# SwiGLU feed-forward: the first loads reordered, and half of the first rows projected before the other half is transposed

## The chip, the cores and the metric

The kernel runs on one core of one Trainium2 chip. The metric is the device time of one execution in microseconds (us), the median over several runs. Beside the times there is one profiled execution of the kernel, whose trace gives the start and the length of every instruction and transfer.

## What is computed

A SwiGLU feed-forward layer in bf16, with x of 2048 rows by 640, w_gate and w_up of 640 by 1536 and w_down of 1536 by 640:

```python
def reference(x, w_gate, w_up, w_down):
    g = silu(x @ w_gate)
    u = x @ w_up
    return (g * u) @ w_down
```

## The kernel before

**Tiles.** The 2048 rows are worked through in four blocks (`sb`) of 512 rows. F = 1536 is cut into 12 slices (`fc`) of 128, and D = 640 into 5 slices (`kd`) of 128. For each block and each `fc`, TensorE projects the transposed block `xT` with the gate slice into a PSUM tile `pg` and with the up slice into `pu`, five matmuls each, one per `kd`, with the weights stationary and 512 columns (rows of x) moving. ScalarE takes SiLU of `pg` into `sg`, VectorE multiplies by `pu` into `aT`. When the 12 slices are done, the block is projected with w_down: `po_t` holds the last 128 output columns transposed, `po_a` the first 512 output columns for each 128 rows. The last block makes the last 128 rows of those columns in `po_b`.

**The start.** For the first block, x comes in four chunks of 128 rows (`x_sb`, chunks 0 to 3) and TensorE transposes it: `transpose_chunk` makes five 128x128 transposes into a PSUM tile `pt`, and a copy brings `pt` to `xT`. Ahead of that TensorE multiplies a tile of ones by itself 20 times (`warm`, tile `pw`); these matmuls, called fillers here, produce nothing that is used. For the other three blocks `xT` is written by transposing transfers.

**Order of the first loads.** Two queues issue transfers, that of SyncE (SP) and that of ScalarE (ACT). Before the change each takes: x chunk (0 on SP, 2 on ACT), x chunk (1 on SP, 3 on ACT), its part of the first gate slice `wg_sb` (kd 0 to 2 on SP, kd 3 and 4 on ACT), its part of the first up slice `wu_sb` in the same way. All further weights go on SP alone: gate and up in chunks of 2, 3, 3 and 3 slices (`W_CHUNKS`), then w_down, then the transposing transfers. Eight semaphores are shared out to the transfers in turn, so the ninth transfer in program order waits at its queue until the first has landed, the tenth for the second, and so on. ScalarE, after its last start transfer, loads its function table (L89) and makes one small SiLU.

**Order on TensorE at the start.** It is written out by hand and held by `keep_order`: 20 fillers; transposes of chunks 0, 2, 1 and 3; two fillers; `pg` for rows 0 to 383; `pg` for rows 384 to 511; `pu` for all 512 rows; then the slices 1 to 11 in the regular form. Three of the chunks are copied to `xT` whole by VectorE, chunk 3 by VectorE (2 of 5 kd) and ScalarE (3 of 5). PSUM has four buffers under the tag `gu` (`pw`, `pg`, `pu`) and two each under `po_a` and `po_b`, which the `pt` tiles of the start borrow.

Of the kernel before, what the change touches and what calls it, by code (L numbers as in the profile page):

```python
# [10 lines left out]
def _body(  # L11
# [8 lines left out]
    nc = tc.nc  # L20
    P = nc.NUM_PARTITIONS
# [5 lines left out]
    B, S0, D = x.shape  # L27
    F = w_gate.shape[1]
    S = B * S0
# [3 lines left out]
    KD = D // P  # L33
    KF = F // P
    S_BLK = 512
    NSB = S // S_BLK
    SUB = S_BLK // P
    DA = 512
    Q = 32
    N_WARM = 20  # L40
    W_CHUNKS = [(0, 1), (1, 3), (3, 6), (6, 9), (9, 12)]
    assert D % P == 0 and F % P == 0 and S % S_BLK == 0 and D > DA and SUB >= 2

    consts = ctx.enter_context(tc.tile_pool(name="consts", bufs=1))
    work = ctx.enter_context(tc.tile_pool(name="work", bufs=3))
# [8 lines left out]
    wg_sb = consts.tile([P, KD, F], bf16)  # L54
    wu_sb = consts.tile([P, KD, F], bf16)
# [7 lines left out]
    wg_v = w_gate.rearrange("(kd p) f -> p kd f", p=P)  # L63
    wu_v = w_up.rearrange("(kd p) f -> p kd f", p=P)
    wd_v = w_down.rearrange("(kf p) d -> p kf d", p=P)

    def wslice(a, b):
        return slice(a * P, b * P)

    def load_w(eng, dst, src, a, b):  # L70
        eng.dma_start(out=dst[:, :, wslice(a, b)], in_=src[:, :, wslice(a, b)])

    def load_x(eng, c0, c1):
        eng.dma_start(out=x_sb[:, c0:c1, :], in_=x_v[:, c0:c1, :])
# [4 lines left out]

    queues = (nc.sync, nc.scalar)  # L80
    halves = ((0, KD // 2 + 1), (KD // 2 + 1, KD))
    for c in (0, 1):
        for i, eng in enumerate(queues):
            load_x(eng, c + 2 * i, c + 2 * i + 1)
    for dst, src in ((wg_sb, wg_v), (wu_sb, wu_v)):
        for eng, (k0, k1) in zip(queues, halves):
            eng.dma_start(out=dst[:, k0:k1, wslice(0, 1)], in_=src[:, k0:k1, wslice(0, 1)])
    load_w(nc.sync, wg_sb, wg_v, *W_CHUNKS[1])
    nc.scalar.activation(silu_first[:], ones[:, 0:1], ACT.Silu)  # L89
    load_w(nc.sync, wu_sb, wu_v, *W_CHUNKS[1])  # L90
    for a, b in W_CHUNKS[2:]:
# [9 lines left out]
    def warm(n):  # L101
        for _ in range(n):
            nc.tensor.matmul(  # L103
                pw[:, 0:P], lhsT=ones[:], rhs=ones[:], start=True, stop=True
            )

    def keep_order(engine):

        traced = [i for i in nc.cur_bb.bb.instructions if i.engine == engine]
        for a, b in zip(traced, traced[1:]):  # L110
            tc.add_manual_dep(
                b,
                a.name,
                mybir.DependencyInfo(
                    mybir.DependencyClass.NoSync, mybir.DependencyReason.DATA
                ),
                reason="keep_order",
            )

    def transpose_chunk(c, parts):  # L120
        c_sl = slice(c * P, (c + 1) * P)
        for copy, tag, k0, k1 in parts:
            pt = psum.tile([P, k1 - k0, P], bf16, tag=tag, name="pt")
            for kd in range(k0, k1):
                nc.tensor.transpose(  # L125
                    out=pt[:, kd - k0, :],
                    in_=x_sb[:, c, kd * P : (kd + 1) * P],
                    identity=ident[:],
                )
            copy(out=xT[:, k0:k1, c_sl], in_=pt[:])  # L130

    def proj(ps, w_sb, fc, sb, c0, c1):
        for kd in range(KD):
            nc.tensor.matmul(  # L134
                ps[:, c0:c1],
                lhsT=w_sb[:, kd, fc * P : (fc + 1) * P],
                rhs=xT[:, kd, sb * S_BLK + c0 : sb * S_BLK + c1],
                start=(kd == 0),
                stop=(kd == KD - 1),
            )  # L140

    for sb in range(NSB):
        s_sl = slice(sb * S_BLK, (sb + 1) * S_BLK)
        for fc in range(KF):
            pg = psum.tile([P, S_BLK], f32, tag="gu", name="pg", bufs=4)
            pu = psum.tile([P, S_BLK], f32, tag="gu", name="pu", bufs=4)
            if sb == 0 and fc == 0:
                h = (SUB - 1) * P
                warm(N_WARM)
                for n, c in enumerate((0, 2, 1)):  # L150
                    transpose_chunk(
                        c, [(nc.vector.tensor_copy, ("po_a", "po_b")[n % 2], 0, KD)]
                    )
                transpose_chunk(
                    SUB - 1,
                    [
                        (nc.vector.tensor_copy, "po_b", 0, 2),
                        (nc.scalar.copy, "po_a", 2, KD),
                    ],
                )  # L160
                warm(2)
                proj(pg, wg_sb, fc, sb, 0, h)
                proj(pg, wg_sb, fc, sb, h, S_BLK)
                proj(pu, wu_sb, fc, sb, 0, S_BLK)
                keep_order(mybir.EngineType.PE)
                keep_order(mybir.EngineType.Activation)
            else:
                proj(pg, wg_sb, fc, sb, 0, S_BLK)
                proj(pu, wu_sb, fc, sb, 0, S_BLK)
            sg = work.tile([P, S_BLK], f32)  # L170
            nc.scalar.activation(sg[:], pg[:], ACT.Silu)  # L171
            nc.vector.tensor_tensor(  # L172
                out=aT[:, fc, s_sl], in0=sg[:], in1=pu[:], op=ALU.mult
            )


        n_t = (SUB if sb < NSB - 1 else SUB - 1) * P
        po_t = psum.tile([P, n_t], f32, tag="po_b", name="po_t")
        for kf in range(KF):
            nc.tensor.matmul(  # L180
                po_t[:],
                lhsT=wd_sb[:, kf, DA:D],
                rhs=aT[:, kf, sb * S_BLK : sb * S_BLK + n_t],
                start=(kf == 0),
                stop=(kf == KF - 1),
            )
        ot_t = outp.tile([P, n_t], bf16, name="ot_t")
        ot_q = outp.tile([P, n_t], bf16, name="ot_q")
        nc.scalar.copy(ot_t[:], po_t[:])  # L189
        nc.vector.transpose(out=ot_q[:], in_=ot_t[:])  # L190
        for q in range(P // Q):
            nc.scalar.dma_start(
                out=out2[
                    sb * S_BLK : sb * S_BLK + n_t, DA + q * Q : DA + (q + 1) * Q
                ].rearrange("(i r) c -> r i c", r=Q),
                in_=ot_q[q * Q : (q + 1) * Q, :].rearrange("r (i c) -> r i c", c=Q),
            )

        for j in range(SUB):
            s0 = sb * S_BLK + j * P  # L200
            last = sb == NSB - 1 and j == SUB - 1
            po_a = psum.tile([P, DA], f32, tag="po_a", name="po_a")
            for kf in range(KF):
                nc.tensor.matmul(  # L204
                    po_a[:],
                    lhsT=aT[:, kf, s0 : s0 + P],
                    rhs=wd_sb[:, kf, 0:DA],
                    start=(kf == 0),
                    stop=(kf == KF - 1),
                )  # L210
            ot = outp.tile([P, DA], bf16, name="ot")
            nc.scalar.copy(ot[:], po_a[:])  # L212
            nc.sync.dma_start(out=out2[s0 : s0 + P, 0:DA], in_=ot[:])
            if last:
                po_b = psum.tile([P, D - DA], f32, tag="po_b", name="po_b")
                for kf in range(KF):
                    nc.tensor.matmul(  # L217
                        po_b[:],
                        lhsT=aT[:, kf, s0 : s0 + P],
                        rhs=wd_sb[:, kf, DA:D],  # L220
                        start=(kf == 0),
                        stop=(kf == KF - 1),
                    )
                ot_b = outp.tile([P, D - DA], bf16, name="ot_b")
                nc.vector.tensor_copy(out=ot_b[:], in_=po_b[:])  # L225
                nc.scalar.dma_start(out=out2[s0 : s0 + P, DA:D], in_=ot_b[:])
# [76 lines left out]
def kernel(tc, *args):  # L303
    _body(tc, *args)
    tc.close()
    tc.compile()
    _trim(tc.nc)
# [30 lines left out]
```

## Time and profile before

| | us |
|---|---|
| median of 8 runs | 164.35 |
| lowest and highest of them | 163.86, 165.48 |
| the profiled execution, its own time | 163.86 |
| its span, first to last instruction | 162.5 |
| TensorE busy | 159.2 (98% of the span) |
| ScalarE busy | 42.2 |
| VectorE busy | 37.9 |

How to read a profile: PE is a matmul on TensorE, PEld a weight load on TensorE, DVE is VectorE, ACT ScalarE, POOL GpSimd, SP SyncE; SPq and ACTq are the issuing of transfers on their queues. In the timeline a line gives start and length of a merged run of equal instructions, then the engine, the line of code, the operation, the tiles out<-in, the shape and the count (x20). Matmuls are pipelined, so the length of one (219 ns for 128 columns, 379 ns for 512) is longer than the distance from one start to the next. The profiled execution is the fastest of the eight; its time has 1.36 us (163.86 less 162.5) outside the span.

### The profile page before, as it was taken

The page shows a single profiled execution, that of the slowest core. Times are in us where ns is not written, and L with a number is a line of the kernel's source. Part 1 is how long each engine was busy: PE and PEld are TensorE (multiplying, and loading weights), DVE is VectorE, ACT ScalarE, POOL GpSimd, SP SyncE. Part 2 cuts the span into 40 slices and gives each one's busy share as a digit, 9 for nine tenths or more (in the row PEclk, how much of TensorE's full clock was granted, in tenths as well). Part 3 has the DMA queues.
Part 4 walks back from the last instruction along what each step waited for, and adds up shares of the span by engine and source line. Part 5 has one row for each costly group of instructions (what it writes and reads, how often), then busy time and mean ns, then how long its engine had stood idle before and what let it go on. Part 6 is the DMA issues. An engine that isn't in the chain of part 4 may idle for free.

```text
span 162.5 us, 1864 instructions
## 1 busy us (share of the span) xinstructions
PE 159.2 (98%) x764; PEld 75.3 (46%) x779; DVE 37.9 (23%) x58; ACT 42.2 (26%) x71; POOL 0.6 (0%) x6
## 2 busy tenths in 40 slices
PE   9999999999999999999999999999999999999994
PEld 8544444444444444444444444444444444445442
DVE  2332233310022233321002333331001333332000
ACT  3222222112222222221222222221223222222121
POOL 1000000000000000000000000000000000000000
DMA  7999999613100000003210000000320000000302
GB/s 220 271 338 331 362 240 199 140 12 86 35 32 0 0 0 0 4 0 33 66 65 0 2 4 0 0 0 6 59 69 32 0 0 0 0 0 4 56 33 73
DMA packets 26888, 11.26 MB, mean 69 GB/s; under 512 B 17664, under 2 KB 26880, under 8 KB 26880
## 3 DMA queue, kind: packets, MB, share of 16 engines
q1 hardware_dynamic: 17968, 10.16, 22.7%
q10 hardware_dynamic: 8912, 0.98, 4.1%
q8 instruction: 6, 0.10, 0.3%
q14 instruction: 2, 0.02, 0.1%
HBM read 6.55 MB, written 2.62 MB: 56 GB/s over the span
## 4 chain that ended last, share of the span: by engine, by line
PE 97%; DVE 1%; issue 1%
PE pg L134 32%; PE pu L134 32%; PE po_a L204 25%; PE po_t L180 6%; PE pw L103 1%; PE pt L125 1%; DVE xT L130 1%; PE po_b L217 0%; DVE ot_b L225 0%; DVE ones L78 0%
## 5 line engine op out<-in xcount | busy, mean ns | idle before, releaser
L134 PE MATMUL pg<-xT,wg_sb 128*128 128x512 bf16 (+2 forms) x245 | 59.7, 375 | 0.1
L134 PE MATMUL pu<-xT,wu_sb 128*128 128x512 bf16 x230 | 59.0, 379 | 0.5
L172 DVE TENSOR_TENSOR aT<-sg,pu 128x512 bf16<-128x512 f32 x48 | 33.1, 689 | 100.8 <-PE pu L134 100.8
L171 ACT ACTIVATE sg<-pg 128x512 f32<-128x512 f32 x48 | 28.7, 597 | 71.0 <-PE pg L134 71.0
L204 PE MATMUL po_a<-wd_sb,aT 128*128 128x512 bf16 x188 | 41.9, 379 | 0.2
L134 PEld LDWEIGHTS <-wg_sb 128*128 128x128 bf16 x245 | 23.7, 98 | 28.4 <-DMA wg_sb<-in_w_gate_dram 0.4
L134 PEld LDWEIGHTS <-wu_sb 128*128 128x128 bf16 x240 | 23.4, 98 | 28.1 <-DMA wu_sb<-in_w_up_dram 0.2
L204 PEld LDWEIGHTS <-aT 128*128 128x128 bf16 x192 | 18.7, 98 | 22.6
L212 ACT CAST ot<-po_a 128x512 bf16<-128x512 f32 x16 | 9.4, 585 | 32.4 <-PE po_a L204 18.7
L180 PE MATMUL po_t<-aT,wd_sb 128*128 128x512 bf16 (+1 forms) x47 | 10.3, 366 | 0.1
L180 PEld LDWEIGHTS <-wd_sb 128*128 128x128 bf16 x48 | 4.7, 98 | 5.1
L189 ACT CAST ot_t<-po_t 128x512 bf16<-128x512 f32 (+1 forms) x4 | 2.2, 558 | 11.7 <-PE po_t L180 11.7
L190 DVE STREAM_TRANSPOSE ot_q<-ot_t 128x512 bf16<-128x512 bf16 (+1 forms) x4 | 2.7, 678 | 9.0 <-ACT ot_t L189 9.0
L103 PE MATMUL pw<-ones 128*128 128x128 bf16 x22 | 2.6, 304 | 0.4 <-DVE ones L78 0.4
L225 DVE CAST ot_b<-po_b 128x128 bf16<-128x128 f32 x1 | 0.3, 291 | 9.9 <-PE po_b L217 9.9
L103 PEld LDWEIGHTS <-ones 128*128 128x128 bf16 x22 | 2.2, 142 | 0.4 <-DVE ones L78 0.4
L130 DVE COPY xT<-pt 128x640 bf16<-128x640 bf16 (+1 forms) x4 | 1.6, 438 | 3.0 <-PE pt L125 2.9
L125 PE MATMUL pt<-ident,x_sb 128*128 128x128 bf16 x20 | 2.1, 284 | 0.0
L125 PEld LDWEIGHTS <-x_sb 128*128 128x128 bf16 x20 | 1.9, 137 | 0.1
L89 ACT ACT_TABLE_LOAD x1 | 1.3, 1283 | 2.1 <-issue 2.1
L217 PEld LDWEIGHTS <-aT 128*128 128x128 bf16 x12 | 0.8, 98 | 0.2
L217 PE MATMUL po_b<-wd_sb,aT 128*128 128x128 bf16 x12 | 0.8, 219 | 0.0
(9 smaller groups left out, 1.7 us busy)
## 6 DMA issues: line engine op xcount, KB each, us to landing
out_dram<-ot SPq DMA_DIRECT2D x16, 128.0 KB, 1.7
wd_sb<-in_w_down_dram SPq DMA_DIRECT2D x1, 1920.0 KB, 11.6
wg_sb<-in_w_gate_dram SPq DMA_DIRECT2D x3, 480.0 KB, 7.6
wu_sb<-in_w_up_dram SPq DMA_DIRECT2D x3, 480.0 KB, 7.7
out_dram<-ot_q ACTq DMA_DIRECT2D x12, 32.0 KB, 1.9
x_sb<-in_x_dram SPq DMA_DIRECT2D x2, 160.0 KB, 2.4
x_sb<-in_x_dram ACTq DMA_DIRECT2D x2, 160.0 KB, 3.0
wg_sb<-in_w_gate_dram SPq DMA_DIRECT2D x1, 320.0 KB, 4.3
```

The source lines that it names most:

```text
L103: nc.tensor.matmul(pw[:, 0:P], lhsT=ones[:], rhs=ones[:], start=True, stop=True)
L125: nc.tensor.transpose(out=pt[:, kd - k0, :], in_=x_sb[:, c, kd * P : (kd + 1) * P], identity=ident[:],)
L130: copy(out=xT[:, k0:k1, c_sl], in_=pt[:])
L134: nc.tensor.matmul(ps[:, c0:c1], lhsT=w_sb[:, kd, fc * P : (fc + 1) * P], rhs=xT[:, kd, sb * S_BLK + c0 : sb * S_BLK + c1], start=(kd == 0 ...
L171: nc.scalar.activation(sg[:], pg[:], ACT.Silu)
L172: nc.vector.tensor_tensor(out=aT[:, fc, s_sl], in0=sg[:], in1=pu[:], op=ALU.mult)
L180: nc.tensor.matmul(po_t[:], lhsT=wd_sb[:, kf, DA:D], rhs=aT[:, kf, sb * S_BLK : sb * S_BLK + n_t], start=(kf == 0), stop=(kf == KF - 1),)
L189: nc.scalar.copy(ot_t[:], po_t[:])
L190: nc.vector.transpose(out=ot_q[:], in_=ot_t[:])
L204: nc.tensor.matmul(po_a[:], lhsT=aT[:, kf, s0 : s0 + P], rhs=wd_sb[:, kf, 0:DA], start=(kf == 0), stop=(kf == KF - 1),)
L212: nc.scalar.copy(ot[:], po_a[:])
L217: nc.tensor.matmul(po_b[:], lhsT=aT[:, kf, s0 : s0 + P], rhs=wd_sb[:, kf, DA:D], start=(kf == 0), stop=(kf == KF - 1),)
```

## The change

The loads are issued in another order: on each queue an x chunk (0 on SP, 1 on ACT), the part of the first gate slice, an x chunk (2 on SP, 3 on ACT), the part of the first up slice. The next gate chunk (slices 1 and 2) is also cut in two parts, kd 0 to 2 on SP and kd 3 and 4 on ACT, so that the ACT queue has a fifth transfer ahead of the table load. On TensorE, after the 20 fillers, chunks 0 and 1 are transposed, three fillers follow, then `pg` is made for rows 0 to 127 and for rows 128 to 255, three more fillers follow, chunks 2 and 3 are transposed, and then come `pu` for rows 0 to 255, `pg` for rows 256 to 511 and `pu` for rows 256 to 511. Chunks 0 and 1 are copied whole by VectorE, chunks 2 and 3 each by ScalarE (2 of 5 kd) and VectorE (3 of 5). Everything from slice 1 on is as it was.

```diff
-    N_WARM = 20
+    N_WARM, N_GAP = 20, 3
...
-    for c in (0, 1):
+    def load_halves(dst, src, a, b):
+        for eng, (k0, k1) in zip(queues, halves):
+            eng.dma_start(out=dst[:, k0:k1, wslice(a, b)], in_=src[:, k0:k1, wslice(a, b)])
+
+    for c, dst, src in ((0, wg_sb, wg_v), (SUB // 2, wu_sb, wu_v)):
         for i, eng in enumerate(queues):
-            load_x(eng, c + 2 * i, c + 2 * i + 1)
-    for dst, src in ((wg_sb, wg_v), (wu_sb, wu_v)):
-        for eng, (k0, k1) in zip(queues, halves):
-            eng.dma_start(out=dst[:, k0:k1, wslice(0, 1)], in_=src[:, k0:k1, wslice(0, 1)])
-    load_w(nc.sync, wg_sb, wg_v, *W_CHUNKS[1])
+            load_x(eng, c + i, c + i + 1)
+        load_halves(dst, src, *W_CHUNKS[0])
+    load_halves(wg_sb, wg_v, *W_CHUNKS[1])
     nc.scalar.activation(silu_first[:], ones[:, 0:1], ACT.Silu)
     load_w(nc.sync, wu_sb, wu_v, *W_CHUNKS[1])
...
-                h = (SUB - 1) * P
+                h = SUB // 2 * P
+                dve, act = nc.vector.tensor_copy, nc.scalar.copy
                 warm(N_WARM)
-                for n, c in enumerate((0, 2, 1)):
-                    transpose_chunk(
-                        c, [(nc.vector.tensor_copy, ("po_a", "po_b")[n % 2], 0, KD)]
-                    )
-                transpose_chunk(
-                    SUB - 1,
-                    [
-                        (nc.vector.tensor_copy, "po_b", 0, 2),
-                        (nc.scalar.copy, "po_a", 2, KD),
-                    ],
-                )
-                warm(2)
-                proj(pg, wg_sb, fc, sb, 0, h)
+                transpose_chunk(0, [(dve, "po_a", 0, KD)])
+                transpose_chunk(1, [(dve, "po_b", 0, KD)])
+                warm(N_GAP)
+                proj(pg, wg_sb, fc, sb, 0, P)
+                proj(pg, wg_sb, fc, sb, P, h)
+                warm(N_GAP)
+                for c in (2, 3):
+                    transpose_chunk(c, [(act, "po_a", 0, 2), (dve, "po_b", 2, KD)])
+                proj(pu, wu_sb, fc, sb, 0, h)
                 proj(pg, wg_sb, fc, sb, h, S_BLK)
-                proj(pu, wu_sb, fc, sb, 0, S_BLK)
+                proj(pu, wu_sb, fc, sb, h, S_BLK)
```

More of the change, by code (lines that the diff above doesn't have):

```diff
@@ L39, in _body @@
     Q = 32
-    N_WARM = 20
+    N_WARM, N_GAP = 20, 3
     W_CHUNKS = [(0, 1), (1, 3), (3, 6), (6, 9), (9, 12)]
-    assert D % P == 0 and F % P == 0 and S % S_BLK == 0 and D > DA and SUB >= 2
+    assert D % P == 0 and F % P == 0 and S % S_BLK == 0 and D > DA and SUB == 4
     consts = ctx.enter_context(tc.tile_pool(name="consts", bufs=1))
```

## The prediction

> **What bounds the kernel now.** First the page's busy times and the chain that ended last.
>
> ```profile
> PE 159.2 (98%) x764; PEld 75.3 (46%) x779; DVE 37.9 (23%) x58; ACT 42.2 (26%) x71; POOL 0.6 (0%) x6
> ...
> PE 97%; DVE 1%; issue 1%
> ```
>
> TensorE sets the end. From slice 1 on the chain in order of time has a step of 1.08 us for each five matmuls without a break (0.216 us each), and the change touches nothing there. So only one number can move: when TensorE comes to slice 1. Hence the second view, the timeline of the first 9 us.
>
> ```profile
> 0.40 2.31 PE L103 MATMUL pw<-ones 128*128 128x128 bf16 x20 [0.40 <-DVE ones L78]
> ...
> 2.05 1.28 ACT L89 ACT_TABLE_LOAD   x1 [2.05 <-issue]
> ...
> 2.50 2.12 PE L125 MATMUL pt<-ident,x_sb 128*128 128x128 bf16 x20
> ...
> 3.28 1.66 DVE L130 COPY xT<-pt 128x640 bf16<-128x640 bf16 x4 [2.94 <-PE pt L125]
> 3.35 0.20 ACT L89 ACTIVATE silu_first<-ones 128x1 f32<-128x1 bf16 x1
> ...
> 4.46 0.27 PE L103 MATMUL pw<-ones 128*128 128x128 bf16 x2
> ...
> 4.66 0.48 ACT L130 COPY xT<-pt 128x384 bf16<-128x384 bf16 x1 [1.11 <-PE pt L125]
> 4.80 1.25 PE L134 MATMUL pg<-xT,wg_sb 128*128 128x384 bf16 x10
> ...
> 6.10 1.03 PE L134 MATMUL pu<-xT,wu_sb 128*128 128x512 bf16 x4
> 7.00 1.25 PE L134 MATMUL pg<-xT,wg_sb 128*128 128x512 bf16 x5
> ```
>
> Slice 1 begins at 7.00. Before it TensorE is hardly idle: the first `pg` matmul starts at 4.80 although the last filler has streamed by 4.57, because the third VectorE copy ends at 4.745 (0.22 us); the fourth chunk of x is 0.12 us late (a transpose that could start at 4.05 starts at 4.17). One `pu` record of five is missing, so the hole ahead of 6.10 is none. Third, the waits of the first 12 us, and the transfers:
>
> ```profile
> PEld L134 <- DMA wg_sb<-in_w_gate_dram: 0.4, 1, 0.4
> ```
> ```profile
> x_sb<-in_x_dram SPq DMA_DIRECT2D x2, 160.0 KB, 2.4
> x_sb<-in_x_dram ACTq DMA_DIRECT2D x2, 160.0 KB, 3.0
> wg_sb<-in_w_gate_dram SPq DMA_DIRECT2D x1, 320.0 KB, 4.3
> ```
>
> The wait is a weight load that runs ahead; the matmuls lose 0.04 us by it (slice 0 has streamed at 6.75 + 0.216 = 6.97, slice 1 starts at 7.00). The 320 KB chunk, issued at 2.63, lands at 6.96. So compute and the slice-1 weights arrive together: whoever shortens one alone meets the other. Single landings in the trace: x at 2.07 and 3.12 (SP), 2.62 and 4.13 (ACT); gate slice 4.49 and 4.88, up slice 5.27 and 5.35; second up chunk 7.88, needed at 8.09. The stretch 2 to 6 us shows 233 to 324 GB/s with the engines' share at 1.05 or more: the transfers are at their limit.
>
> Pace: up to 4.00 the starts of 128-column matmuls lie 0.107 us apart, after that 0.056. 384 columns take 0.162, 512 take 0.216.
>
> **The change part by part.**
>
> *Fillers and transposes.* The first 20 fillers stay (0.40 to 2.50). Chunks 0 and 1: ten transposes at 0.107 = 1.07, to 3.57; chunk 1 now takes the place of chunk 2 (landing 2.62) and is needed at 3.03. Three fillers at 0.107 = 0.32, to 3.89. They cover the copy of chunk 0 (3.28 to 3.77, plus 0.05 to the matmul as at 4.745 to 4.80, so 3.82); they overshoot it by 0.07.
>
> *`pg` for rows 0 to 255.* Rows 0 to 127: one matmul at 0.107 and four at 0.056, 3.89 to 4.22. The copy of chunk 1 runs 3.81 to 4.31 as its counterpart does now, so rows 128 to 255 start at 4.36 after a wait of 0.14, end 4.64. Three fillers at 0.056: 4.81.
>
> *Chunks 2 and 3.* Ten transposes at 0.056 instead of 0.107 and 0.056 mixed: 5.37.
>
> *The other three quarters.* No 256-column matmul is in the trace; between 0.056 and 0.162 the middle is 0.109, which I take. `pu` rows 0 to 255: 5 x 0.109, to 5.91; `pg` second half to 6.46; `pu` second half to 7.00. Slice 0 then has streamed at 7.00 instead of 6.97. The bounds on the 256-column pace (0.108, half of 512, to 0.112, twice 128) are 0.0 to +0.05 over 15 matmuls.
>
> *Copies, who waits.* VectorE copies of 640, 256 elements take 0.492 and 0.278, so 384 about 0.35. Chunk 2's three end 5.25 (last start 5.03 + 0.22), copy 5.29 to 5.64; chunk 3's copy 5.68 to 6.03. The third `pg` matmul of the second half, which waits for it, is due at 6.13: spare 0.05. ScalarE has 0.478 for 384, so about 0.36 for 256: 5.12 to 5.48 and 5.48 to 5.84, needed at 5.91: spare 0.02 after the 0.05. If either slips by 0.1, the end slips by up to 0.1.
>
> *The ACT queue.* The fifth transfer there waits for chunk 1 (2.62), issues in 0.37 to 0.53 as the rows do; behind it stand the table load, the first SiLU and the two copies. Table load 3.1 to 4.4, SiLU to 4.6; ScalarE is wanted at 5.1. Cost nothing, covered by TensorE's transposes up to 5.09; without that cover each us costs one. The Trainium skill (ScalarE: Activation LUTs, section What ACT_TABLE_LOAD costs) speaks against the change: about 1283 ns for the load and some 1380 ns of drain. The row has the 1283 ns, but the SiLU starts 0.012 us after it, with no drain. By the page ScalarE would come free at about 6.0 and the sum would grow by 0.8 us, an estimate; I go by the row.
>
> *Arrivals.* Up to the gate slice and all of x the bytes are the same in both orders (800 KB), so the last of these still lands by 4.88; the gate parts, now second on their queues, between 2.62 and 4.13 (the second x chunks there now, which are larger), needed at 3.89 and 4.06; x chunks 2 and 3 between 3.12 and 4.88, needed at 4.81 and 5.09; up slice as now 5.27 and 5.35, needed at 5.37 and 5.70. Late ends cost 0.07 on the gate part, which the copy wait of 0.14 swallows, and 0 elsewhere; early ends gain nothing, as TensorE is due later. The 320 KB chunk: SP's part may issue at 2.07 and ACT's at 2.62 instead of 2.63, but 960 KB stand ahead of it in both orders. Early end 5.9 (first engine's landing now), which gains 0 because compute is due at 7.00; late end 7.88 (the chunk behind it), which costs 0.88. I take 6.96, nearest by bytes. On SP the next up chunk waits for the gate's ACT part, about 0.5 us later than its issue at 3.05 now; SP's queue holds unmoved work until after 5, so it costs 0. Behind it, later chunks have over 1 us of spare (10.13 landed against 11.3 needed).
>
> *Sum in the profiled execution:* 7.00 against 7.00, plus up to 0.1 for copies: +0.0 to +0.1, so 163.9.
>
> *From there to the median.* The profiled run is 0.49 below the median 164.35, and the trace does not say what the others lose. If it is the slow pace lasting longer, the change costs a bit more: four more fillers at 0.107 = 0.43, less the 0.12 wait for x, is 0.31 at slow pace, worth 0.31 x 0.056/0.107 = 0.16 once the pace turns. So +0.0 to +0.2, middle +0.1: 164.45. The Trainium skill (TensorE: Matmul & The Clock Gate, section Part 1) says that the window which turns the clock up runs freely and does not start with the kernel; by its 3.4 us, half of it lost, runs would differ by up to 1.7 us, an estimate near the 1.62 between lowest and highest here. The profile's clock column has 1.00 throughout, so only the distances of starts show the pace.
>
> **The rivals.**
>
> *ScalarE comes late (slower).* The table load now starts a us later, behind a transfer that waits for a landing. If load, issue and landing together stretch, the copies of chunks 2 and 3 are late and TensorE stands ahead of `pg` second half. It decides from ScalarE free at about 5.1; at 6.0 the two copies end at 6.7 and the end moves by 0.85, so 165.2; at 6.5, 165.7. Against it: 0.5 us of spare by the rows, and the load had 1.28 in the midst of full transfers.
>
> *The split chunk lands late (slower within the range).* If turns between the queues bring the gate chunk down with the up chunk behind it, slice 1 waits until up to 7.88: +0.9 at most, +0.3 if a third of it comes true.
>
> *Loads hide better (faster).* If what the median loses against the profile is late x, the projection of rows 0 to 255 hides it: up to the 0.49 and the 0.34 of idle named above, 164.35 - 0.83 = 163.5. Against it: the bytes ahead of slice 1 are the same, and its weights stand at 6.96 either way.
>
> *The early projection hides nothing:* that is my forecast, since TensorE was already full; what it gains in idle (0.34 against 0.14) it spends on four more fillers.
>
> **How the numbers follow.** Forecast with its neighbours of small size 0.75, own range 164.2 to 164.8. Slower by the ScalarE wait or the whole late chunk 0.14; faster by late x 0.11. About 0.5% (0.82 us) is what a measurement can tell from no change: below 163.53 faster, above 165.17 slower. The range takes half of each rival's reach and the spread of a median: 163.7 to 165.2.
>
> **What would show it.** In the changed profile: first `pg` matmul at 3.9; a wait of about 0.14 on the copy of chunk 1; ten transposes 4.8 to 5.4 at the fast pace; slice 1 at 7.0 to 7.1; table load at about 3.1 and ScalarE's first copy at 5.1. Wrong if slice 1 starts before 6.6 or after 7.6, if a weight load waits over 0.3 us for the split chunk, or if ScalarE's copies start after 5.6.

## The result and the profile after

The changed kernel takes 165.01 us (median of 17 runs, 163.96 to 165.42) against 164.25 us (47 runs); the ratio is 1.0045, 95% interval 1.0034 to 1.0056. It is slower by 0.45%, some 0.7 us.

The profiled execution took 165.25 us with a span of 163.9, which is 1.39 us more than the profile before. That is about twice the difference of the medians, since the profile before is 0.39 us below its median and this one 0.24 us above. First its chain that ended last, from the page, by engine and by line:

```profile
PE 95%; DMA 3%; issue 1%; SPq 0%; DVE 0%
PE pu L136 32%; PE pg L136 31%; PE po_a L203 25%; PE po_t L179 6%; DMA x_sb<-in_x_dram 3%; PE pt L127 1%; PE po_b L216 0%; SPq L84 0%; SPq L74 0%; DVE ot_b L224 0%
```

A transfer stands in it that was not there before: x, with 3% of the span. The timeline of the first 10 us shows where:

```profile
2.61 1.25 PE L127 MATMUL pt<-ident,x_sb 128*128 128x128 bf16 x10
...
3.52 1.28 ACT L91 ACT_TABLE_LOAD   x1 [3.52 <-DMA x_sb<-in_x_dram]
...
3.98 1.27 PE L136 MATMUL pg<-xT,wg_sb 128*128 128x128 bf16 x10
...
4.81 0.20 ACT L91 ACTIVATE silu_first<-ones 128x1 f32<-128x1 bf16 x1
...
5.04 0.53 PE L105 MATMUL pw<-ones 128*128 128x128 bf16 x3
...
5.91 0.84 PE L127 MATMUL pt<-ident,x_sb 128*128 128x128 bf16 x10 [0.34 <-DMA x_sb<-in_x_dram]
...
6.76 0.72 PE L136 MATMUL pu<-xT,wu_sb 128*128 128x256 bf16 x5
...
7.87 0.71 PE L136 MATMUL pu<-xT,wu_sb 128*128 128x256 bf16 x5
...
8.63 1.03 PE L136 MATMUL pg<-xT,wg_sb 128*128 128x512 bf16 x4
```

The last line lacks its first record (four of five), so slice 1 starts at 8.63 - 0.22 = 8.41 instead of 7.00. That is the whole difference between the two profiles: from slice 1 on, every multiplication into `aT` comes 1.40 us later than before, to the end. Within it, the transposes of chunk 2 start at 5.91, where the working had 4.81. The waits of the first 9.5 us and the transfers (median from issue to landing) name the cause:

```profile
PEld L127 <- DMA x_sb<-in_x_dram: 0.8, 2, 0.6
PE pt L127 <- DMA x_sb<-in_x_dram: 0.3, 1, 0.3
PEld L136 <- DMA wu_sb<-in_w_up_dram: 0.2, 1, 0.2
```
```profile
x_sb<-in_x_dram SPq DMA_DIRECT2D x2, 160.0 KB, 3.8
x_sb<-in_x_dram ACTq DMA_DIRECT2D x2, 160.0 KB, 4.0
```

Before, x took 2.4 and 3.0 us from issue to landing. Chunks 2 and 3 now land at 5.87 and 6.12. In the trace each transfer has 16 landings, one for each of the core's 16 transfer engines, and it is complete with the last of them; 14 of the 16 had finished chunk 2 by 4.12, the last two at 4.80 and 5.87. There is a second difference: TensorE's 128-column matmuls lie 0.107 us apart until 6.1, where before the pace turned to 0.056 between 4.00 and 4.17. So two theories stand against each other. A: the new order of the loads brings x and the up slice late. B: TensorE's own new order, with its holes, holds back the turn of the pace.

### The profile page after: what moved, and what is told of

It is laid out like the page before. It is cut to its first block, busy times and chain, and to the rows that moved or that the text cites. A ratio compares the mean times of both kernels' runs of the same rounds, so it can differ in the third digit from the quotient of the medians.

```text
span 163.9 us, 1895 instructions
## 1 busy us (share of the span) xinstructions
PE 160.4 (98%) x779; PEld 76.8 (47%) x793; DVE 37.8 (23%) x58; ACT 42.4 (26%) x72; POOL 0.6 (0%) x6
## 3 DMA queue, kind: packets, MB, share of 16 engines
q10 hardware_dynamic: 9184, 1.12, 4.3%
HBM read 6.55 MB, written 2.62 MB: 56 GB/s over the span
## 4 chain that ended last, share of the span: by engine, by line
PE 95%; DMA 3%; issue 1%; SPq 0%; DVE 0%
PE pu L136 32%; PE pg L136 31%; PE po_a L203 25%; PE po_t L179 6%; DMA x_sb<-in_x_dram 3%; PE pt L127 1%; PE po_b L216 0%; SPq L84 0%; SPq L74 0%; DVE ot_b L224 0%
## 5 line engine op out<-in xcount | busy, mean ns | idle before, releaser
L136 PE MATMUL pu<-xT,wu_sb 128*128 128x512 bf16 (+1 forms) x245 | 59.8, 375 | 0.0
L136 PEld LDWEIGHTS <-wg_sb 128*128 128x128 bf16 x250 | 24.5, 100 | 27.6
L105 PE MATMUL pw<-ones 128*128 128x128 bf16 x26 | 3.4, 313 | 0.4 <-DVE ones L78 0.4
L105 PEld LDWEIGHTS <-ones 128*128 128x128 bf16 x26 | 2.8, 148 | 0.4 <-DVE ones L78 0.4
L132 ACT COPY xT<-pt 128x256 bf16<-128x256 bf16 x2 | 0.7, 372 | 1.3 <-PE pt L127 1.3
```

The costliest lines, as they stand in the source:

```text
L105: nc.tensor.matmul(pw[:, 0:P], lhsT=ones[:], rhs=ones[:], start=True, stop=True)
L136: nc.tensor.matmul(ps[:, c0:c1], lhsT=w_sb[:, kd, fc * P : (fc + 1) * P], rhs=xT[:, kd, sb * S_BLK + c0 : sb * S_BLK + c1], start=(kd == 0 ...
```

## The experiments

Ratios are to the kernel before, run beside each, with the 95% interval in brackets. The pace is the distance from one matmul's start to the next.

**The changed kernel once more** (no edit).

> The changed kernel unchanged, for a second profile beside these runs. Theory A: x chunks 2 and 3 land after 4.5 again, the up slice after 5.5, second up chunk at 8.5 or later; ratio 1.0034 to 1.0056. Theory B: the turn of the pace is later than 5.4 again; if it is near 4.9 as with nine fillers, the turn varies from run to run by itself.

164.88 us, ratio 1.0040 (1.0025 to 1.0054). Its profiled execution took 165.26 us, as long as the first, but the pace turned at 3.64. Its timeline and its waits:

```profile
3.82 0.96 PE L136 MATMUL pg<-xT,wg_sb 128*128 128x128 bf16 x10
...
4.61 0.33 PE L105 MATMUL pw<-ones 128*128 128x128 bf16 x3
...
5.93 0.56 PEld L127 LDWEIGHTS <-x_sb 128*128 128x128 bf16 x10 [1.16 <-DMA x_sb<-in_x_dram]
...
6.70 0.72 PE L136 MATMUL pu<-xT,wu_sb 128*128 128x256 bf16 x5
```
```profile
PEld L127 <- DMA x_sb<-in_x_dram: 1.2, 1, 1.2
PE pt L127 <- DMA x_sb<-in_x_dram: 1.0, 1, 1.0
```

This separates the theories for these two executions of the changed kernel. With the turn 2.5 us earlier TensorE reaches its second fillers 0.4 us sooner and only waits longer: chunk 2 lands at 5.88 and sets the rest. The sum closes to 0.03: 5.93 less 4.81 is 1.12, a wait of 0.2 for the up slice (landed 6.66) follows, and slice 1 starts at 8.35 (the first record is missing again), which is 1.35 later than before. Both profiled executions are slower than their medians, by 0.24 and 0.38 us, so a median run loses less than they do.

**Each half of the change alone.** First the new loads with the old order on TensorE.

```diff
-                transpose_chunk(0, [(dve, "po_a", 0, KD)])
-                transpose_chunk(1, [(dve, "po_b", 0, KD)])
-                warm(N_GAP)
-                proj(pg, wg_sb, fc, sb, 0, P)
...
+                for n, c in enumerate((0, 1, 2)):
...
+                warm(2)
+                proj(pg, wg_sb, fc, sb, 0, h)
                 proj(pg, wg_sb, fc, sb, h, S_BLK)
+                proj(pu, wu_sb, fc, sb, 0, S_BLK)
```

> The new loads (order and split) with the old order on TensorE: all four chunks transposed (0, 1, 2, 3), two fillers, then slice 0 as before. Theory A (transfers): x chunks 2 and 3 come at about 5.9 and 6.1 as in the changed kernel, so slice 0 starts at about 6.4 and slice 1 at about 8.6; ratio to the kernel before about 1.009. Theory B (pace of TensorE alone: the new order breaks its stream, transfers do not matter): transposes end near 4.6, slice 1 at 7.0 to 7.2, ratio 1.000 to 1.001.

166.5 us, ratio 1.0111 (1.0072 to 1.0149). Its timeline:

```profile
2.58 1.25 PE L127 MATMUL pt<-ident,x_sb 128*128 128x128 bf16 x10
5.21 1.25 PE L127 MATMUL pt<-ident,x_sb 128*128 128x128 bf16 x10 [1.38 <-DMA x_sb<-in_x_dram]
...
6.51 2.30 PE L136 MATMUL pg<-xT,wg_sb 128*128 128x384 bf16 x10
9.02 0.47 PE L136 MATMUL pu<-xT,wu_sb 128*128 128x512 bf16 x1 [0.22 <-issue]
...
9.97 0.38 PE L136 MATMUL pg<-xT,wg_sb 128*128 128x512 bf16 x1
```

TensorE's order is the old one, apart from the chunks' sequence, and still the transposes of chunk 2 wait until 5.21, for a chunk that landed at 5.17. So x comes late without TensorE's new order, as theory A has it (with 5.9). A's ratio of 1.009 lies in the interval. But the profile is that of the slowest of the six runs (164.75 to 166.81), and in it slice 1 starts at 9.97 where A had 8.6: the slow pace lasts until about 9.1, and ten `pg` matmuls take 2.30 us instead of 1.25. The ratio holds both the late x and a late turn of the pace, and B is not excluded as a part of it.

Then the old loads with the new order on TensorE.

```diff
-    for c, dst, src in ((0, wg_sb, wg_v), (SUB // 2, wu_sb, wu_v)):
...
+    for c in (0, 1):
+        for i, eng in enumerate(queues):
+            load_x(eng, c + 2 * i, c + 2 * i + 1)
...
+    load_w(nc.sync, wg_sb, wg_v, *W_CHUNKS[1])
```

> The old loads (x 0 and 2, x 1 and 3, gate slice, up slice, second gate chunk whole on SP) with the new order on TensorE. Theory A (the new order of the loads makes the transfers slower): x lands by 4.2, gate slice by 4.9, up slice by 5.4, second up chunk near 7.9 as before; TensorE now waits for the gate slice at 3.9 to 4.5 and then runs through, slice 1 at 7.7 to 8.0 by the same working as in the prediction; ratio 1.003 to 1.005, from the order alone. Theory B (pace): TensorE's idle time of 0.6 at 3.9 delays the turn to 6 or later, slice 1 at 8.2 or later, ratio 1.006 or more. If the order were harmless, ratio 1.000.

165.08 us, ratio 1.0079 (1.0044 to 1.0114). The ten runs fall in two groups, six from 164.57 to 165.16 and four from 166.52 to 166.72. The profiled one (165.16):

```profile
3.87 0.53 PE L103 MATMUL pw<-ones 128*128 128x128 bf16 x3
4.75 1.15 PE L134 MATMUL pg<-xT,wg_sb 128*128 128x128 bf16 x10 [0.35 <-DMA wg_sb<-in_w_gate_dram]
5.74 0.33 PE L103 MATMUL pw<-ones 128*128 128x128 bf16 x3
...
8.32 1.03 PE L134 MATMUL pg<-xT,wg_sb 128*128 128x512 bf16 x4
```

Now x is early (chunk 3 at 3.87) and the gate slice (4.70 and 4.80) is what TensorE waits for. The pace turned at about 5.7, and slice 1 starts at 8.10 (its first record is missing), between A's 8.0 and B's 8.2. The ratio is one that B forecast, by the four runs of the upper group; the six of the lower group average 164.81, 0.6 us above the kernel before, which is what A forecast. What makes the groups is open (see the last section). Each half puts a wait in TensorE's way, for x in the one and for the gate slice in the other, and neither half alone was faster than the kernel before.

**The split of the second gate chunk.** Alone on the kernel before:

```diff
-    load_w(nc.sync, wg_sb, wg_v, *W_CHUNKS[1])
+    for eng, (k0, k1) in zip(queues, halves):
+        eng.dma_start(out=wg_sb[:, k0:k1, wslice(*W_CHUNKS[1])], in_=wg_v[:, k0:k1, wslice(*W_CHUNKS[1])])
```

> The kernel before with the split of the second gate chunk over both queues as the only edit. Theory A with the order of the first transfers as cause: x, gate and up slices land as before, slice 1 at 7.0, ratio 0.999 to 1.001. If the split is a part of the cause: the gate chunk or the up chunk behind it lands later than 7.1 and 8.1, slice 1 waits, ratio 1.002 or more.

164.21 us, ratio 1.0001 (0.9984 to 1.0018): no difference. Its two parts landed at 6.16 and 6.57, ahead of the 6.96 of the whole; the profile shows another wait in its place, for a gate slice that came at 5.01 in that execution:

```profile
5.05 1.27 PE L135 MATMUL pg<-xT,wg_sb 128*128 128x384 bf16 x10 [0.43 <-DMA wg_sb<-in_w_gate_dram]
...
7.24 1.24 PE L135 MATMUL pg<-xT,wg_sb 128*128 128x512 bf16 x5
```

And taken out of the changed kernel:

```diff
-    load_halves(wg_sb, wg_v, *W_CHUNKS[1])
+    load_w(nc.sync, wg_sb, wg_v, *W_CHUNKS[1])
```

> The changed kernel with the second gate chunk whole on SP again, so ACT's fifth transfer is gone. If the split is what makes x chunks 2 and 3 late (theory A with the split as cause), they land by 4.9, TensorE's wait of 0.55 us goes, ratio about 1.001. If the order of the first eight transfers is the cause (theory A) or the pace (theory B), the ratio stays at 1.004 to 1.005; the table load moves back to about 2.1 in every case.

164.7 us, ratio 1.0034 (1.0017 to 1.0052). x chunks 2 and 3 landed at 5.13 and 5.35, the table load was back at 2.04. So x is late without the split too, and the split, with the later table load that comes with it, is not what makes the kernel slower.

**The fillers in the gaps.** Nine instead of three ahead of chunk 2:

```diff
                 proj(pg, wg_sb, fc, sb, P, h)
-                warm(N_GAP)
+                warm(9)
                 for c in (2, 3):
```

> The changed kernel with nine fillers instead of three ahead of chunk 2, so TensorE has work through the wait of 0.55 us (six fillers at 0.107 are 0.64). Theory A: the wait is only filled, slice 1 at 8.4 to 8.5, ratio 1.004 to 1.006. Theory B with idle time as what delays the turn from 0.107 to 0.056: the turn comes at about 4.0 to 5.4 instead of 6.1, slice 0 is not much earlier in its start but runs fast throughout, ratio 1.002 to 1.004.

164.96 us, ratio 1.0039 (1.0020 to 1.0057). In this profile x came early (4.47 and 4.89), TensorE never waited for it, and the nine fillers and a turn of the pace at about 5.0 were the delay: slice 1 starts at 7.66 (7.88 less 0.22 for a missing record), where A had 8.4 to 8.5. Then the second up chunk (landed 9.01) held it. The turn and the ratio are those that theory B forecast, but the two profiles of the changed kernel show that the turn moves by itself, from 6.1 to 3.64, so this profile does not show that the fillers brought it on. The lines:

```profile
4.96 0.67 PE L105 MATMUL pw<-ones 128*128 128x128 bf16 x9
5.47 0.72 PE L127 MATMUL pt<-ident,x_sb 128*128 128x128 bf16 x10
...
7.88 1.03 PE L136 MATMUL pg<-xT,wg_sb 128*128 128x512 bf16 x4
9.06 0.39 PE L136 MATMUL pu<-xT,wu_sb 128*128 128x512 bf16 x1 [0.15 <-DMA wu_sb<-in_w_up_dram]
```

None in either gap:

```diff
-    N_WARM, N_GAP = 20, 3
+    N_WARM, N_GAP = 20, 0
```

> The changed kernel without the six fillers in the two gaps. Theory A: the fillers only fill waits for x, ratio 1.003 to 1.005 as with them. Fillers as cause (the prediction's 0.16 to 0.3 us): ratio 1.002 to 1.003. Theory B (idle time delays the turn): more idle time, ratio 1.006 or more.

164.84 us, ratio 1.0038 (1.0020 to 1.0055), the same as with six fillers and below B's 1.006. The fillers cost nothing that can be measured.

**Idle time ahead of the pace's turn**, on the kernel before:

```diff
-    N_WARM = 20
+    N_WARM = 12
```

> The kernel before with 12 first fillers instead of 20: TensorE idles from about 1.7 to the landing of x chunk 0 near 2.1. Theory B (idle time delays the turn of the pace): the turn comes later than 4.0, by up to 2 us, ratio 1.003 to 1.006. If idle time does not matter: the transposes start 0.4 earlier, are held by chunk 3 at 4.1 as now, ratio 0.998 to 1.000.

164.36 us, ratio 1.0014 (0.9991 to 1.0036): inconclusive. TensorE idled from 1.6 to 2.48 and the pace turned at 5.9 in that profile, 2 us later than in the profile of before; slice 1 was 0.5 us later (7.50, the first record missing). So a late turn by 2 us goes with about 0.5 us in the old order in this one profile, but the medians don't show that idle time causes it.

**Why x comes late.** The landing of the last of 16 engines, in us, from the traces:

| loads, kernel | x chunk 2 | x chunk 3 | gate slice | up slice | second up chunk |
|---|---|---|---|---|---|
| old, before | 2.62 | 4.13 | 4.88 | 5.35 | 7.88 |
| old, 12 fillers | 2.85 | 3.85 | 4.67 | 5.33 | 7.9 |
| old, split alone | 2.81 | 3.75 | 5.01 | 5.58 | 7.9 |
| old, new TensorE order | 2.81 | 3.87 | 4.80 | 5.32 | 8.1 |
| new, changed kernel | 5.87 | 6.12 | 3.72 | 6.72 | 8.7 |
| new, changed kernel again | 5.88 | 6.14 | 3.51 | 6.66 | 8.5 |
| new, old TensorE order | 5.17 | 5.42 | 3.58 | 5.99 | 9.0 |
| new, no split | 5.13 | 5.35 | 3.50 | 6.06 | 8.9 |
| new, nine fillers | 4.47 | 4.89 | 3.53 | 5.62 | 9.0 |
| new, no gap fillers | 5.18 | 5.47 | 3.65 | 6.10 | 8.4 |

With the old loads all of x and the gate slice are there by 4.67 to 5.01, with the new ones by 4.89 to 6.14, and all that follows is late with them. From the first engine to the last, chunks 2 and 3 spread over 0.3 to 0.8 us with the old loads and over 1.0 to 2.3 us with the new ones. In the two profiles of the changed kernel 12 of the 16 engines have chunk 2 by 4.03 and 4.21, so it is two to four engines that lag by 0.6 us or more. The transfers as a whole are hardly slower: up to 6.0 us the engines moved 1.41 MB in the kernel before and 1.32 and 1.35 MB in the two profiles of the changed one (from the GB/s of these stretches), where x, gate slice and up slice are 0.98 MB together. Bytes of later transfers went ahead while some of x was still out: the first engine had its part of the second gate chunk at 5.24 and 5.21, before x was complete.

Three edits of the changed kernel ask what makes them lag. Larger rows in the gate slice:

```diff
-        load_halves(dst, src, *W_CHUNKS[0])
-    load_halves(wg_sb, wg_v, *W_CHUNKS[1])
+        load_halves(dst, src, 0, 2 if dst is wg_sb else 1)
+    load_halves(wg_sb, wg_v, 2, 3)
```

> The changed kernel with the first gate chunk two slices wide (rows of 512 bytes instead of 256, 320 KB instead of 160) and the second one slice wide. If small rows of the gate slice ahead of them are what holds some engines back on x chunks 2 and 3, their landings draw together: first engine near 4.1, last by 4.9, the 160 KB more being about 0.5 us for all; ratio 1.001 to 1.003. If not, the spread from first to last engine stays at 1 us or more and the last lands at 5.4 or later; ratio 1.004 or more.

164.92 us, ratio 1.0036 (1.0020 to 1.0052). Chunks 2 and 3 landed at 5.57 and 5.81, 1.7 and 1.5 after their first engines: larger rows did not draw the landings together in this profile.

Nothing queued behind x (first diff), and only the up slice behind it (second diff); the order on SP is held by `keep_order` in both:

```diff
-        load_halves(dst, src, *W_CHUNKS[0])
-    load_halves(wg_sb, wg_v, *W_CHUNKS[1])
+        if dst is wg_sb:
+            load_halves(dst, src, *W_CHUNKS[0])
+    hold = consts.tile([P, 2, 128], bf16)
+    nc.sync.dma_start(out=hold[:], in_=x_sb[:, 2:4, 0:128])
+    load_w(nc.sync, wu_sb, wu_v, *W_CHUNKS[0])
+    load_w(nc.sync, wg_sb, wg_v, *W_CHUNKS[1])
```
```diff
-    load_halves(wg_sb, wg_v, *W_CHUNKS[1])
+    hold = consts.tile([P, 2, 128], bf16)
+    nc.sync.dma_start(out=hold[:], in_=x_sb[:, 2:4, 0:128])
+    load_w(nc.sync, wg_sb, wg_v, *W_CHUNKS[1])
```

> The changed kernel, but the up slice and all later weights go on SP alone behind a small transfer that waits for x chunks 2 and 3, so nothing runs beside those. If transfers queued behind x (the up slice and the second gate chunk) hold some engines back on it, x chunks 2 and 3 land within 0.4 us of each other's first engine, by 4.3; if the order of what lies ahead is the cause, the last engine still comes at 4.9 or later. The time is no measure here: the up slice lands at 6 or later, ratio 1.006 or more in both cases.

> The changed kernel with the up slice in its place, but every later weight on SP alone behind a small transfer that waits for x chunks 2 and 3. If the second gate chunk, running beside x, is what holds engines back on it, x chunks 2 and 3 land by 5.0 as with nothing behind them (4.78 and 4.96); if the up slice or the order ahead does it, they land at 5.1 to 6.1 as in five of the six profiles with the new loads. The second gate chunk lands at 7.5 or later, so slice 1 starts at 7.6 or later and the ratio is 1.004 or more in both cases.

With nothing behind: chunks 2 and 3 at 4.78 and 4.96 (167.40 and 170.34 us in two runs; the profile is of the second, with a granted clock of 0.98, and only its landings are read). That misses the 4.3 of the one forecast and is at the edge of the other (4.9 or later), and the engines still spread over 1.0 and 0.9 us; it is about where the prediction had the last of x (4.88). With the up slice alone behind: 4.94 and 5.13, with 15 of 16 engines there by 4.47 and 4.81; 167.34 us, ratio 1.0174 (1.0134 to 1.0214), as all later weights wait. Both are earlier than the two profiles of the changed kernel (5.9 and 6.1), but with everything behind it the kernel with nine fillers had 4.47 and 4.89. So traffic behind x may add up to 1.2 us; a single profile each does not settle it. Why some engines lag stays open.

**A candidate:** x chunk 0 and the whole gate slice on SP, x chunks 1 to 3 on ACT.

```diff
+    load_x(nc.sync, 0, 1)
+    load_x(nc.scalar, 1, 2)
+    load_w(nc.sync, wg_sb, wg_v, *W_CHUNKS[0])
+    load_x(nc.scalar, 2, 3)
+    load_x(nc.scalar, 3, 4)
+    load_halves(wu_sb, wu_v, *W_CHUNKS[0])
+    load_halves(wg_sb, wg_v, *W_CHUNKS[1])
...
-                warm(2)
-                proj(pg, wg_sb, fc, sb, 0, h)
+                proj(pg, wg_sb, fc, sb, 0, 2 * P)
+                proj(pg, wg_sb, fc, sb, 2 * P, h)
```

> A candidate: x chunk 0 and the whole gate slice on SP, x chunks 1 to 3 on ACT, then up slice and second gate chunk split; TensorE as in the kernel before but chunks in the order 0 to 3, no fillers after the transposes, and pg in rows 0 to 255, 256 to 383, 384 to 511. If the engines share out turns evenly, x and gate slice land by 4.2 and slice 1 starts at 6.6 to 6.9, ratio 0.997 to 0.999. If x on ACT is held back as in the changed kernel (theory A), slice 1 starts after 7.1, ratio 1.000 or more.

164.96 us, ratio 1.0068 (1.0036 to 1.0099). Again TensorE waited for x, for chunk 2 and once more for chunk 3 (landed 4.29 and 5.61). The profile is of one of four runs near 166.7 us; the other eight took 164.51 to 165.16.

```profile
2.63 1.25 PE L129 MATMUL pt<-ident,x_sb 128*128 128x128 bf16 x10
4.34 0.71 PE L129 MATMUL pt<-ident,x_sb 128*128 128x128 bf16 x5 [0.46 <-DMA x_sb<-in_x_dram]
5.66 0.71 PE L129 MATMUL pt<-ident,x_sb 128*128 128x128 bf16 x5 [0.60 <-DMA x_sb<-in_x_dram]
6.17 2.34 PE L138 MATMUL pg<-xT,wg_sb 128*128 128x256 bf16 x15
```

No version that beats the kernel before was found.

## Why the prediction was right, and which step of it failed

The measured time, 165.01, lies in the range (163.7 to 165.2) near its upper end; the change of +0.45% is inside the 0.5% that was called no change, as the likeliest case had it. But the forecast of 164.45 with its own range of 164.2 to 164.8 was too low, and not by chance, and the prediction's own signs of being wrong came: slice 1 after 7.6 (8.41 and 8.35), and ScalarE's copies after 5.6 (6.34 and 6.25), these because x was late. That the range holds is in part luck: its upper end was opened for a late ScalarE and a late split chunk, and neither came; the delay came from a term that the working put at 0.

*The step that failed is the arrivals.* "Up to the gate slice and all of x the bytes are the same in both orders (800 KB), so the last of these still lands by 4.88" bounds the sum of the bytes, and not the engine that is last. Chunks 2 and 3 were to land between 3.12 and 4.88; they landed from 4.47 to 6.14 in six profiles. "Late ends cost 0.07 ... and 0 elsewhere" became 1.1 us for x and 0.2 for the up slice in the two profiles of the changed kernel. Why the last engines lag stays open.

*What was right.* TensorE was nearly full before the change (0.34 us idle) and had little to gain. `pg` started at 3.98 and 3.82 (forecast 3.9), ten transposes at the fast pace took 0.56, 256-column matmuls lie 0.109 apart as taken, and the split chunk never held TensorE.

*ScalarE.* The rival that forecast a late ScalarE did not come: SiLU ended at 5.02 (forecast 4.6; chunk 1 of x landed at 3.08 instead of 2.62), the copies were wanted only at 6.34. The second table load measured is again 1.283 us, and the SiLU starts 0.011 us behind it. The Trainium skill (ScalarE: Activation LUTs, section What ACT_TABLE_LOAD costs) has some 1380 ns of drain beside the load for every switch to another set; no profile here, with one load each, shows it.

*The fillers.* The 0.16 us for four more at the slow pace can't be seen: without any in the gaps the ratio is 1.0038, with six 1.0040 in the same comparison. But 0.16 us is 0.1%, less than the intervals tell apart.

*Faster by late x hidden* did not come: x was complete by 4.13 in the profile before, and the new loads made it late. With the new loads the early projection may well hide a part of that (ratio 1.0045 and 1.0040 with it, 1.0111 without it, though a late turn of the pace has a share in the last), but not enough to win.

## What to carry to other kernels

Equal bytes ahead of a transfer do not mean equal arrival: read the landing on the last of the 16 engines, and take the spread between first and last engine (here 1.0 to 2.3 us with the new loads) into the range when the order of small loads changes. Where compute and loads arrive together, as here, cutting the work finer to start earlier moved the wait to whatever was then last; each half of such a change should be costed with the landing it would have if the slowest engine stays behind. A profile whose pace differs from another's explains nothing until a second profile of the same kernel shows whether the time follows it.

## What the hardware showed

The lag of a few engines was not expected: 14 of 16 had chunk 2 at 4.12, then 4.80 and 5.87 in one profile, 12 of 16 at 4.21 and the last at 5.88 in the next. The Trainium skill (DMA: Bandwidth & Descriptors, section Why a DMA increments its semaphore by 16 and not by 1) says that the engines finish independently and that only the full count means that all has landed; the 16 landings in these traces agree, and no row here says why the last ones lag.

The turn of TensorE's pace came at 3.64 and 6.1 in two profiles of the same kernel. The Trainium skill (TensorE: Matmul & The Clock Gate, Part 1) says that it depends on a window that runs freely; that agrees. Its Part 4 says that the full clock does not engage for transposes. Here it does run during them: in the profile before, the pace turned in the midst of the transposes, between 4.00 and 4.17 after 15 of 20, and in the second profile of the changed kernel eight of ten starts follow at 0.055 to 0.056 us. Fillers ran ahead of the transposes in every profile, so no run shows whether transposes alone would bring it on.

The runs of three kernels fell in two groups some 1.7 us apart: old loads with the new order, 164.57 to 165.16 and 166.52 to 166.72; x on ACT, 164.51 to 165.16 and 166.52 to 166.82; new loads with the old order, 164.75 and 165.38 and then 166.39 to 166.81. The two profiles that come from an upper group (166.69 and 166.81) have the slow pace until about 9.1; the one from a lower group (165.16) has it until 5.7. Another 3.4 us at 0.107 instead of 0.056 would cost 1.6 us, an estimate, which is about the distance of the groups. That the pace makes the groups is argued from these three profiles and not tested. A hole in TensorE's work does not suffice for it: the first profile of the changed kernel has one of 0.55 us just ahead of its turn at 6.1, and none of that kernel's runs went above 165.57; and one run of the kernel before took 166.77.
